# Projecting V as a transposed product and turning it in 32x32 blocks on VectorE

## The chip, the cores and the metric

The kernel runs on one core of a Trainium2 chip. The metric is the device time of one execution in microseconds. A run is one execution; where several are given, the median is compared. The profile is of one execution.

## The reference

The input is x of 2048 rows (tokens) by 512 features in bf16. The result is two rounds of an attention block A and a token-mixing MLP block B, each with a layer norm in front and a residual sum behind:

```python
x = x + A(layernorm(x), wqkv, wo)
x = x + B(layernorm(x), w1, b1, w2, b2)
x = x + A(layernorm(x), wqkv, wo)
x = x + B(layernorm(x), w1, b1, w2, b2)

def A(x, wqkv, wo):        # 32 heads of 16 features, a window of 256 keys behind each query
    q, k, v = split((x @ wqkv).reshape(B, S, 3, H, Dh))
    scores = einsum("bhqd,bhkd->bhqk", q, k) * Dh ** -0.5
    scores = where(0 <= iq - ik < 256, scores, -1e9)
    return einsum("bhqk,bhkd->bhqd", softmax(scores), v).reshape(B, S, D) @ wo

def B(x, w1, b1, w2, b2):  # mixes over tokens
    u = gelu(einsum("bsd,sf->bdf", layernorm(x), w1) + b1)
    return (einsum("bdf,fs->bds", u, w2) + b2).transpose(0, 2, 1)
```

## The kernel before

All tensors of a round lie in the on-chip memory; weights of B are streamed. The 2048 tokens are 16 tiles of 128, and the attention goes through them in four blocks Q of 512 queries. In a block the 32 heads come in four groups t of eight heads, and a group takes nine steps m. So there are 144 steps in a round, 36 for a block and 9 for a group. One step does three things:

- `emit_scores` (L743): products of 64x64 pieces on TensorE for all eight heads, 512 queries, into two banks of PSUM. Two pairs of banks take turns.
- `emit_exp` (L754, L771): ScalarE writes the exponentials of the two banks to one of five slots of `p_sb`; then VectorE or GpSimd multiplies the stretches at the edge of the window with a triangular mask, `edge`.
- `emit_pv` (L792): products of the slot with V on TensorE. Each piece of V has two columns of ones beside it, so the sums of the softmax come out of the same product.

Around the steps stand jobs: `job_transpose` (L554) makes `xhT`, the normalised x with features on partitions; `job_k` and `job_q` (L565, then L606 on VectorE or L611 on ScalarE) project one group of heads for a whole block in four products of 128x128 by 512 and write a masked copy twice, since two heads share a piece; `job_v` (L659) projects V; `job_normalise` (L835, L842) and `job_outproj` (L708) finish a block. The MLP follows (L931, L977); parts of it (`job_part` and the late half of `job_y`, both L581) are put between attention steps.

V is needed with keys on partitions. `job_v(Q, i)` takes one tile of 128 tokens and all 32 heads. Its keys are handled as four groups of 32, and each group is put on partitions 32a to 32a+31 in a product 32 columns wide, so it consists of 64 small products:

```python
last = e.matmul(acc[32 * a:32 * a + 32, k], lhsT=xhT[:, buf, c, t0:t0 + 32], rhs=wv[:, c, :, a, :],
                start=(k == 0 and c == 0), stop=(k == 3 and c == 3), skip_group_check=True,
                tile_position=(0, 32 * a))
```

The bank then holds V for the tile, and one instruction (`masked`: VectorE L606, or two of ScalarE L611) writes it to `v_all`, twice, each time with the partitions of the other heads set to zero by `even`. The jobs' results other than scores and P times V go through two banks of PSUM, 6 and 7 (`misc_bank`).

The order is fixed by tables written out in the kernel: `ORDER` gives the order in which jobs are made, `BANKS` which of the two banks each takes, and `LINES` the exact order of the instructions on each engine. Semaphores do the rest. The first product of P and V in a block waits for what `v_held(Q)` lists: all four tiles of V of that block.

Of the kernel before, what the change touches and what calls it, by code (L numbers as in the profile page):

```python
# [6 lines left out]
dt = mybir.dt  # L7
# [3 lines left out]
P = 128  # L11
# [18 lines left out]
def _table(*text):  # L30
# [5 lines left out]
    'c-pO0!4`lp2onDPqw7$sUg?l!uS1h^FeoAd$IZCcxtcv+t9kXhHM);~qfow6_xQqT^Xo}4wX1n`Su(*gRlcwNx(bk{aKei+``iKU`E$QuyVvts'  # L36
    'w(s>^P)Z~wimbDAvd6)jpPkI@c<da4Ua)cj`@e^2n!S|i3DnSRo!7T}wJfXoUUwnKS75UHw>BeK0EP')
ORDER = _table(
    'c-jTQ17HvU00h8Cwq47%ZQHhOyS8lGwr$(CZ5wxhK!isy7$FcGp%4xs5f%{<29Xg7Q4s^75fiZy0gVs^aS;pAkpOWJAMua~(U1a(kr2s|6iE<('
    ')JTSuNP|>Ji)_e%^vH~K$cRkHiY&;E+{lT1$br1bg*+&Lq9}y?D2T!+h9WqKk|>ALD1qWAg|euKGANHqsDR3-hN`H78fb=ksEOLBj#{XLy6A}p'  # L40
    '=#D0+kH%<<hG>qCXoHq$f&OTXR%nL~Xp0_bk1iOE&gh0t=#8!zf~Dw-UKofzn1}%wj6n3mBn(9mM&KxBU>HVW5QbwU#$q)lU<}4%9HwF)rehhV'
    'U^ZrA8s=dRW?>=bVgVLmF(zXLmSYu`U?tXIEjD2TPGd9HV<XmK3$|iDc3?NQV;gp2FLq%M4&eYUU_XxFI1b|xj^QL8<1DV>6i(ng&fpv_;u3D-'
    'Dz4x%uHy!7;U@0kA@1TnKHv@>;3b~o1)ktJUg0&!XLyIVc#n_xjyC|m;4?nq8$$CJzTzi-;4l6m4ioYZej_+TF&NV`B+YOP!LW?PFwDa6jK+wJ'
    '%E*kxxQx#DjKP?U#{kA=0w$uEgvpqgDH(xDnVQL&ifNgSDOi}9nT8pdi5Z!bQJ9T6n3dU?i)ERcd6|y|n1}gUkcHTWMOlQ!Se%Vmf+bm+rC5eN'
    'Sf15biRD<4RXB##S(!Cil{HwG^;m%o*?_g!ly%sg_1T1t*_zGRg00w&ZP}6?*_j>Kon6_9eb|k?*^lkni~Tu}gV~ouIDkDF#GxF{VI09h9L;eY'
    '#R(kCNgU5<oXDx1&OpxKOwQtD&gE<_;6hH}d@kl9F5yzH;Bv0wTCU_8uIFlQ;70D`O>W|5-rzFs<s9zgHE!W`ZsR)M=3Q>(E#BcS?&c0|=N=y5'
    'exBwT9^@gO<vE_<DW2p-9_JAr<6)lXQC{W+Ug0I)<9%M`BR=K>KH)>Y=2L#=3%=wlKI3zK<a@s1TfXBLe&8p5=MVlN^o>9Ho4@##e`y8RKZaB='
    'Q6Uscp(TY=7)4N6MN)W0R1`&30>xA`MOQ3ERvZN=hGHw8;wq66D!Gy<gOVw+k}9P#Dz#E5y;3Qiax04pE0eM+r?RVodMdASD8KS3pGv8aifVug'
    's<?`%m`bRmnyZW^s-jA(sw$|8YN)bmtGeoHnrf-O>ZqO?s*xHizFMk@+N-r%sGYK@mD;MK(yD_xDYLq$fO4sudZ?PZs=IorlKQH*YO0_5sJwzy'
    'PJ=Z_!xX5Y8llk|sb-p>&g!r68mCDbqox|7Hkzy{ny#r@uNhjbS(>L6nyCevqxo8>MH;B3TB2oIuHjm#)mp1{+MrRItBu;E&Dx@!+M%u5u3g%u'  # L50
    '+1jVwI-tGUqeI%SgF2#PI;#6Ru2Wj0GditvI<Lbzs}s7UtGb|zx~VI=u4_7}Te_{gx}nRuqlbE;M|z;AdZy>Pr#JebS9+=UdaX}-thbWi>7%~u'
    'g+A+>e(RUM>aYIkhrZ~Kf;*T)7!K($ro;ND5<9%ZIf5fOv?DsIqd2-lIkN3oj^?<I=@^df1dikQ4saqTaSA7NQYUvhr*<-@avG;~O2=~sr*|f2'
    'b}naeMrU(Y=Wr3{aYg5JcIS3J7jl00a~&6OQ5SS^7j{dRbupK88JBkjS8`34a1~c~HP?1k*K%Fgb3-?9V>fa$H+Nn)b$hpR8<%!DcW`TWc3Zb|'
    '3s-hGcXU_RaCi4`Pxo>s_jMol_W%!apa*)G2YZBvdbmfrzDIeq$9jUhILPBY(UUycV?5PUJl!)q#IrotGd;(%y}<Lm(#O5fi+s$Bebm#u*7Ll?'
    '>wLn?e9C9M)F*w~tG(PSyvl35(Yw9go4m&xyx04@#hbm=+q}y=yxj-9)BAnUhkeLLeAX9z&R2ZFmwegheciYG%(s2V_kGU~eACzb*f)IDcm3Rt'
    '{L~Nq(og)tZ~V%y{U4S=?Gg')
# [1054 lines left out]
```

## Time and profile before

| | |
|---|---|
| Three runs | 506.96, 507.89 and 508.72 us; median 507.89 |
| Profiled execution | 508.97 us, of it 507.2 in the span of the profile |
| TensorE (PE), busy | 489.2 us, 96%, 10374 products and as many weight loads |
| VectorE (DVE), busy | 320.3 us, 63%, 615 instructions |
| ScalarE (ACT), busy | 325.3 us, 64%, 396 instructions |
| GpSimd (POOL), busy | 189.2 us, 37%, 390 instructions |
| V products, L659 | 2048 of them, 34.8 us busy |

Times in rows are microseconds, those behind a count ("x26 | 31.5, 1215") are the group's busy time in microseconds and the mean of one in nanoseconds. "PEld" is TensorE's weight load, which runs beside the products. "idle before <- X" is the time that the engine stood still before such an instruction and what ended it; "issue" means that nothing which the profile shows held it. The first attention lies at about 10 to 170 us, the first MLP at 165 to 235, the second attention at 235 to 420, the second MLP after that. The granted clock was 1.00 but for a stretch in the slice from 30 to 40 us, where it was 0.83.

### The profile page before, as it was taken

How to read it: one execution, taken by the hardware profiler on the slowest of the kernel's cores; microseconds unless marked ns; L12 is line 12 of the kernel's file. 1: busy time of each engine (PE TensorE's matmuls, PEld its weight loads, DVE VectorE, ACT ScalarE, POOL GpSimd, SP SyncE). 2: the span in 40 equal slices, each digit the busy share in tenths (PEclk: the TensorE clock that was granted, in tenths of full speed). 3: DMA queues.
4: the chain of work that ended last, by engine and by line, in shares of the span. 5: the costliest groups of instructions: out<-in, count | busy, mean ns of one | idle time of the engine just before them, and what ended most of it. 6: DMA issues, size and time to landing. Idle time of an engine off the chain costs nothing.

```text
span 507.2 us, 23041 instructions
## 1 busy us (share of the span) xinstructions
PE 489.2 (96%) x10374; PEld 288.6 (57%) x10374; DVE 320.3 (63%) x615; ACT 325.3 (64%) x396; POOL 189.2 (37%) x390
## 2 busy tenths in 40 slices
PE   8989999899999999999999998998999999999997
PEld 4655756665676544446665665566556654444444
DVE  7879888789755472257868476777785556342223
ACT  4869999898999514404897568787999871240000
POOL 5856645643745120002564133465473322100000
PEclk9989999999999999999999999999999999999999
DMA  6362212141031555031000320014212356222551
GB/s 207 65 70 63 64 44 69 59 132 45 5 109 54 158 152 145 2 108 40 4 26 5 98 78 17 14 41 125 77 45 70 88 141 197 68 78 70 183 152 52
DMA packets 70769, 40.81 MB, mean 80 GB/s; under 512 B 7056, under 2 KB 69648, under 8 KB 70672
## 3 DMA queue, kind: packets, MB, share of 16 engines
q1 hardware_dynamic: 66800, 39.33, 26.4%
q0 software_dynamic: 3872, 0.02, 1.3%
q8 instruction: 81, 1.33, 1.1%
q14 instruction: 16, 0.13, 0.1%
HBM read 32.51 MB, written 2.10 MB: 68 GB/s over the span
## 4 chain that ended last, share of the span: by engine, by line
PE 84%; DVE 5%; ACT 4%; issue 3%; DMA 1%; POOL 1%; SPq 0%; DVEq 0%; POOLq 0%; ACTq 0%
PE ps L977 14%; PE ps L743 12%; PE ps L931 12%; PE ps L792 10%; PE ps L581 10%; PE ps L565 9%; PE ps L659 6%; PE ps L708 5%; ACT p_sb L754 4%; PE ps L554 2%; PE ps L506 1%; PE ps L835 1%; DVE k_sb L606 1%; DMA w1low<-in_B_w_dram 1%; DVE oT L842 1%
## 5 line engine op out<-in xcount | busy, mean ns | idle before, releaser
L754 ACT ACTIVATE p_sb<-ps 128x1024 bf16<-128x1024 f32 (+8 forms) x288 | 261.8, 974 | 45.0 <-PE ps L743 40.1
L771 POOL TENSOR_TENSOR p_sb<-p_sb,edge 128x256 bf16<-128x256 bf16 (+2 forms) x294 | 138.4, 476 | 161.9 <-ACT p_sb L754 141.7
L743 PE MATMUL ps<-q_sb,k_sb 64*64 64x288 bf16 (+8 forms) x2816 | 109.4, 250 | 6.3 <-issue 3.6
L792 PE MATMUL ps<-p_sb,v_all 64*34 64x288 bf16 (+17 forms) x2816 | 88.5, 246 | 1.1 <-issue 0.5
L743 PEld LDWEIGHTS ps<-q_sb,k_sb 64*64 64x64 bf16 x2816 | 58.3, 106 | 49.9 <-ACT p_sb L754 24.0
L792 PEld LDWEIGHTS ps<-p_sb,v_all 64*34 64x34 bf16 (+1 forms) x2816 | 60.7, 101 | 11.3 <-POOL p_sb L771 2.9
L565 PE MATMUL ps<-xhT,wqkv 128*128 128x512 bf16 x240 | 62.0, 384 | 0.0
L981 DVE SCALAR_TENSOR_TENSOR x_sb<-ps,b2col,x_sb 128x512 bf16<-128x512 f32 x23 | 17.2, 750 | 44.4 <-PE ps L977 44.1
L931 PE MATMUL ps<-xh_sb,w1buf 128*128 128x512 bf16 x192 | 44.8, 379 | 0.0
L771 DVE TENSOR_TENSOR p_sb<-p_sb,edge 128x256 bf16<-128x256 bf16 (+2 forms) x106 | 28.1, 268 | 25.8 <-ACT p_sb L754 22.3
L524 POOL TENSOR_TENSOR rstd<-vare,mhalf 128x4 f32<-128x4 f32 (+1 forms) x17 | 16.6, 976 | 71.6 <-DVE vare L522 47.7
L512 DVE BATCH_NORM_STATS2 stats<-x_sb 128x6 f32<-128x512 bf16 x64 | 42.8, 684 | 0.8
L534 ACT ACTIVATE xh_sb<-x_sb,shift,rstd 128x512 bf16<-128x512 bf16 x18 | 14.2, 808 | 44.2 <-POOL shift L528 29.1
L606 DVE TENSOR_TENSOR k_sb<-ps,half 128x1024 bf16<-128x1024 f32 (+1 forms) x29 | 34.2, 1183 | 10.8 <-PE ps L565 8.0
L977 PE MATMUL ps<-ubuf,w1buf 128*128 128x512 bf16 x168 | 37.7, 379 | 0.0
L606 DVE TENSOR_TENSOR q_sb<-ps,even 128x1024 bf16<-128x1024 f32 (+1 forms) x28 | 33.4, 1196 | 6.5 <-PE ps L565 5.3
L659 PE MATMUL ps<-wqkv,xhT 128*32 128x128 bf16 x2048 | 34.8, 220 | 2.6 <-issue 1.8
L606 DVE TENSOR_TENSOR v_all<-ps,even 128x1024 bf16<-128x1024 f32 x26 | 31.5, 1215 | 6.1 <-PE ps L659 5.7
L977 PE MATMUL ps<-ubuf,oU 128*128 128x512 bf16 x154 | 35.0, 379 | 0.0
L581 PE MATMUL ps<-xh_sb,w1low 64*64 64x512 bf16 x512 | 33.9, 377 | 0.8 <-DMA w1low<-in_B_w_dram 0.8
L938 ACT ACTIVATE ubuf<-ps,b1col 128x512 bf16<-128x512 f32 x28 | 18.8, 686 | 23.7 <-DVE ps L936 14.3
L659 PEld LDWEIGHTS ps<-wqkv,xhT 128*32 128x32 bf16 x2048 | 29.1, 97 | 8.5 <-issue 4.8
(80 smaller groups left out, 499.9 us busy)
## 6 DMA issues: line engine op xcount, KB each, us to landing
w1buf<-in_B_w_dram SPq DMA_DIRECT2D x30, 256.0 KB
w1buf<-in_B_w_dram SPq DMA_DIRECT2D x50, 128.0 KB
oU<-in_B_w_dram SPq DMA_DIRECT2D x18, 256.0 KB
oU<-o SPq DMA_DIRECT2D x16, 256.0 KB
w1low<-in_B_w_dram SPq DMA_DIRECT2D x32, 128.0 KB
xhT<-in_B_w_dram SPq DMA_DIRECT2D x4, 512.0 KB
k_sb<-in_B_w_dram SPq DMA_DIRECT2D x4, 512.0 KB
out_dram<-x_sb SPq DMA_DIRECT2D x15, 128.0 KB
```

What stands on the lines that cost most here:

```text
L512: dve(lambda e: e.bn_stats(stats[:, t, :], x_sb[:, t, :]), 690, prio, reads=[R("x", t)], writes=[R("stats", t)])
L565: last = e.matmul(ps[:, b, :], lhsT=wqkv[:, c, c0:c0 + P], rhs=xhT[:, buf, c, :], start=(c == 0), stop=(c == 3))
L581: last = e.matmul(ps[64 * h:64 * h + 64, banks[r ^ swap], :], lhsT=lhs(r ^ swap, c, rows, 64 * h), rhs=rhs(r ^ swap, c, rows), start=(c == ...
L606: return e.tensor_tensor(dst, src.unsqueeze(2).to_broadcast([P, n, 2, w]), mask[:].unsqueeze(1).unsqueeze(3).to_broadcast([P, n, 2, w]), o ...
L659: last = e.matmul(acc[32 * a:32 * a + 32, k], lhsT=xhT[:, buf, c, t0:t0 + 32], rhs=wv[:, c, :, a, :], start=(k == 0 and c == 0), stop=(k = ...
L708: last = e.matmul(ps[:, b, :], lhsT=oT[:, buf, t, i * P:(i + 1) * P], rhs=wo_sb[:, t, :], start=(t == 0), stop=(t == 3))
L743: last = e.matmul(ps[64 * c:64 * c + 64, 2 * half + r, 32 * i0:32 * i1], lhsT=k_sb[rows, ring, t, kb % 16, :], rhs=q_sb[rows, t, c, 32 * i ...
L754: exps[plan.job] = last_exp[0] = plan.op({ACT: (170 + int(2 * (512 - c0) * 0.84), lambda e: e.activation(p_sb[:, slot, :, c0:512], ps[:, 2 ...
L771: return e.tensor_tensor(v, v, g, op=ALU.mult)
L792: last = e.matmul(ps[64 * r:64 * r + w, B_O + (c ^ r), 32 * i0:32 * i1], lhsT=v_all[rows, pos - 32 * c:pos - 32 * c + w], rhs=p_sb[rows, s ...
L931: r = e.matmul(ps[:, b, :], lhsT=blk[:, sc - 8 * part, (ft % 2) * P:(ft % 2 + 1) * P], rhs=xh_sb[:, sc, :], start=(sc == 8 * part), stop=( ...
L977: r = e.matmul(ps[:, b, :], lhsT=blk[:, turn[n], (st % 2) * P:(st % 2 + 1) * P], rhs=u_at(turn[n]), start=(n == 0), stop=(n == NFT - 1))
```

## The change

`job_v(Q, t)` now takes one group of heads for all 512 tokens of a block, as the K and Q jobs do: four products of 128x128 by 512, with features of V on partitions. VectorE then turns the bank in blocks of 32x32 into a float32 tile `vt`, after which keys lie on partitions, and a second instruction writes the masked double copy from `vt` to `v_all`. It may be on VectorE, ScalarE or GpSimd. So that heads come out in the right places, the columns of V's weights are put in another order once: they are loaded into `ubuf`, and eight copies (`permute_wv`) write them to `wqkv`. `v_all` is laid out by groups of heads, and a PV step waits only for V of its own group (`v_held(Q, t)`). In a block's list of jobs V stands at other places, and three of the four V jobs of a block stand inside that block instead of the one before it. `ORDER`, `BANKS` and `LINES` are new as a whole.

```diff
-        v_all = sb("v_all", [P, 30 + (NV * 8 + 1) * VW])
+        VR = 30 + (2 * NV + 1) * VW
+        v_all = sb("v_all", [P, 4 * VR])
+        vt = sb("vt", [P, 2, 512], dt.float32)
...
+        wv_raw = ubuf[:, 0:4 * D].rearrange("p (c n) -> p c n", c=4)
...
-            load(wqkv[:, :, c * D:(c + 1) * D], w_src[:, :, c * D:(c + 1) * D], 1 << 19, -100, writes=[R("wqkv", c)])
+            part = wqkv[:, :, c * D:(c + 1) * D] if c < 2 else wv_raw
+            load(part, w_src[:, :, c * D:(c + 1) * D], 1 << 19, -100, writes=[R("wqkv", c)] if c < 2 else [R("uT", 0), R("uT", 1)])
...
+        def permute_wv(t, prio):
+            cs = slice(t * P, (t + 1) * P)
+            dst = wqkv[:, :, 2 * D + t * P:2 * D + (t + 1) * P].rearrange("p c (a r d) -> p c a r d", r=2, a=4)
+            src = wv_raw[:, :, cs].rearrange("p c (r a d) -> p c a r d", r=2, a=4)
+            for r in range(2):
+                plan.op({DVE: (260, lambda e, r=r: e.tensor_copy(dst[:, :, :, r], src[:, :, :, r])),
+                         POOL: (560, lambda e, r=r: e.tensor_copy(dst[:, :, :, r], src[:, :, :, r])),
+                         ACT: (390, lambda e, r=r: e.activation(dst[:, :, :, r], src[:, :, :, r], ACTF.Copy))},
+                        reads=[R("uT", 0), R("uT", 1)], writes=[R("wv", t)], prio=prio)
...
-        def job_v(Q, i, prio):
+        def job_v(Q, t, prio):
...
-                for k in range(4):
-                    for c in range(4):
-                        for a in range(4):
-                            t0 = i * P + 32 * k
-                            last = e.matmul(acc[32 * a:32 * a + 32, k], lhsT=xhT[:, buf, c, t0:t0 + 32], rhs=wv[:, c, :, a, :],
-                                            start=(k == 0 and c == 0), stop=(k == 3 and c == 3), skip_group_check=True,
-                                            tile_position=(0, 32 * a))
+                for c in range(4):
+                    last = e.matmul(ps[:, b, :], lhsT=wv[:, c], rhs=xhT[:, buf, c, :], start=(c == 0), stop=(c == 3))
                 return last
...
+            turned = dve(lambda e: e.transpose(vt[:, k, :], ps[:, b, :]), 650, prio, shares=[BK(b)], writes=[R("vt", k)])
+            turned.swap = tuple(turned.deps)
+            g0 = 16 * Q % NV
+            for lo, hi in ((0, min(16, NV - g0)), (min(16, NV - g0), 16)):
...
+                def both(e, dst=dst, src=src, n=n):
+                    return e.tensor_tensor(dst, src.unsqueeze(2).to_broadcast([P, n, 2, DH]),
+                                           even[:].unsqueeze(1).unsqueeze(3).to_broadcast([P, n, 2, DH]), op=ALU.mult)
+
+                def each(e, dst=dst, src=src):
+                    for h in range(2):
+                        last = e.activation(dst[:, :, h], src, ACTF.Copy, scale=even[:, h:h + 1])
+                    return last
+                plan.op({DVE: (80 + 34 * n, both), ACT: (230 + 33 * n, each), POOL: (150 + 52 * n, both)},
+                        reads=[R("vt", k), R("even")], writes=[R("v", t, (g + j) // 4) for j in range(0, hi - lo, 4)], prio=prio)
...
-            order = ["k1", "q1", "v0", "v1", "k2", "q2", "v2", "o0", "k3", "q3", "o1", "v3", "K0", "Q0", "o2", "o3"]
+            order = ["k1", "q1", "v1", "k2", "q2", "v2", "k3", "q3", "o0", "o1", "v3", "K0", "Q0", "V0", "o2", "o3"]
...
-                order = ["k1", "q1", "k2", "q2", "k3", "o0", "q3", "o1", "o2", "o3"]
+                order = ["k1", "q1", "v1", "k2", "q2", "v2", "k3", "o0", "q3", "v3", "o1", "o2", "o3"]
...
-        def v_held(Q):
-            first = 4 * Q - 3 if Q > 0 else 0
-            return [R("pad"), R("ones", 0)] + [R("ones", 129)] * (Q > 0) + [R("v", g % (NV // 4)) for g in range(first, 4 * Q + 4)]
+        def v_held(Q, t):
+            slots = [g % NV for g in range(max(0, 16 * Q - 12), 16 * Q + 16, 4)]
+            return [R("pad"), R("ones", 0)] + [R("ones", 33)] * (Q > 0) + [R("v", t, g // 4) for g in slots]
```

192 lines of the change are left out of this document (99 added, 93 removed).

## The prediction

> **What bounds the kernel now.** I read the chain of work that ended last first, then the busy times by stage, then the waits of TensorE.
>
> ```profile
> span 507.2 us, 23041 instructions
> ...
> PE 84%; DVE 5%; ACT 4%; issue 3%; DMA 1%; POOL 1%; SPq 0%; DVEq 0%; POOLq 0%; ACTq 0%
> ```
>
> TensorE carries 84% of the chain, so the time is its work plus its gaps. The stages that hold the V jobs follow (columns: window, its length, busy us of each engine with the count of instructions, granted clock, DMA share, GB/s).
>
> ```profile
> 40.00:140.00 100.00, 96.98 (x2842) 62.02 (x2843) 85.27 (x147) 92.56 (x107) 56.45 (x112) 1.00 0.21 62
> ...
> 300.00:360.00 60.00, 54.65 (x1760) 36.80 (x1756) 44.66 (x82) 48.16 (x53) 29.25 (x53) 1.00 0.16 45
> ```
>
> In the first attention TensorE, ScalarE and VectorE (97, 93 and 85 of 100 us) are all near their limits, so work moved between them has a price; GpSimd (56) has room. From 300 to 360 us TensorE is at 54.65 of 60 and no other engine is full: those are gaps. The waits of TensorE's loads and products (us in total, times, longest):
>
> ```profile
> PEld ps L743 <- ACT p_sb L754: 24.0, 61, 0.8
> ...
> PEld ps L792 <- POOL p_sb L771: 2.9, 10, 0.4
> ```
>
> ```profile
> PE ps L743 <- issue: 3.6, 3, 1.7
> ...
> PE ps L659 <- issue: 1.8, 4, 0.8
> ...
> PE ps L835 <- issue: 1.2, 1, 1.2
> ...
> PE ps L792 <- issue: 0.5, 1, 0.5
> ```
>
> Two things stand out: scores wait for ScalarE to free their banks, often and briefly; and a few long gaps end by nothing that the profile shows, 3.6 + 1.8 + 1.2 + 0.5 = 7.1 us in nine gaps.
>
> **The products of V.** The slot that a job takes on TensorE is read from the start of its weight loads to the start of the next job's, in the timeline:
>
> ```profile
> 105.03 0.90 PEld L659 LDWEIGHTS ps<-wqkv,xhT 128*32 128x32 bf16 x64
> 106.03 0.21 PEld L743 LDWEIGHTS ps<-q_sb,k_sb 64*64 64x64 bf16 x12
> ...
> 109.40 0.55 PEld L565 LDWEIGHTS ps<-xhT,wqkv 128*128 128x128 bf16 x4 [0.20 <-issue]
> 110.37 0.14 PEld L743 LDWEIGHTS ps<-q_sb,k_sb 64*64 64x64 bf16 x8 [0.42 <-issue]
> ```
>
> ```profile
> 118.97 0.97 PE ps L565 x4
> 119.94 0.86 PE ps L708 x4
> ```
>
> The V job of today takes 1.00 us. A job of four full products, the new form, takes 0.97, or 0.86 where it follows another full-array job (the rows of the chain). A listing of the new program's instructions puts 32 such jobs in place of the old, about nine of them next to another full-array job, either before or after: 32 x 0.03 + 9 x 0.11 = 1.9 us saved. Bounds are 1.0 (no neighbour counts) and 32 x 0.14 = 4.5.
>
> **The gaps called issue.** A V job is 64 loads and 64 products in 1.00 us, the densest code of the kernel. The instruction queue's row (packets, MB, share), and TensorE's products around 307 us in the timeline:
>
> ```profile
> q8 instruction: 81, 1.33, 1.1%
> ```
>
> ```profile
> 304.88 0.57 PE L659 MATMUL ps<-wqkv,xhT 128*32 128x128 bf16 x28
> 305.76 1.58 PE L659 MATMUL ps<-wqkv,xhT 128*32 128x128 bf16 x100 [0.31 <-issue]
> 307.27 0.41 PE L743 MATMUL ps<-q_sb,k_sb 64*64 64x288 bf16 x8
> 307.51 0.61 PE L792 MATMUL ps<-p_sb,v_all 64*34 64x224 bf16 x16
> 307.95 0.19 PE L743 MATMUL ps<-q_sb,k_sb 64*64 64x32 bf16 x4
> 309.49 0.40 PE L743 MATMUL ps<-q_sb,k_sb 64*64 64x288 bf16 x8 [1.35 <-issue]
> ```
>
> 1.33 MB in 81 packets is 16.4 KB each; over 2 x 10374 instructions of TensorE it is 64 bytes an instruction, so a packet brings 256. Between the two gaps here (0.31 and 1.35 us) lie 100 + 8 + 16 + 4 = 128 products, which with their loads are 256 instructions: the second gap falls exactly one packet behind the first. I read both as TensorE waiting for its program. With the change 2 x 2048 instructions become 2 x 128, 18.5% of the stream, and 256 of them no longer go by in two or three microseconds. The gaps beside the normalisation (L835, 1.2) stay, and some in L743 may. I take 4.5 of the 7.1 us, with bounds 0 and 7.1. The Trainium skill, "Runtime: NRT & Kernel Launch", section "Instruction fetch mechanics", says that programs are streamed in 16 KiB blocks and that crossing a block is "mostly hidden" behind the issue of instructions; by it nothing would be gained here, and the sum below would be -0.4 us instead of -4.9. The rows above do not look hidden; the rule is a rival below.
>
> **ScalarE at the start of a round.** These are masks of V that ScalarE does between the first exponentials:
>
> ```profile
> 13.84 1.27 ACT L611 ACTIVATE v_all<-ps,even 128x512 bf16<-128x512 f32 x2 [0.76 <-PE ps L659]
> ...
> 17.32 1.27 ACT L611 ACTIVATE v_all<-ps,even 128x512 bf16<-128x512 f32 x2 [0.29 <-PE ps L659]
> ...
> 20.01 1.29 ACT L611 ACTIVATE v_all<-ps,even 128x512 bf16<-128x512 f32 x2
> ...
> 237.45 1.27 ACT L611 ACTIVATE v_all<-ps,even 128x512 bf16<-128x512 f32 x2 [0.18 <-PE ps L659]
> ```
>
> Four tiles of V had to be there before the first PV; now one group is enough, and in the new order two V jobs instead of four stand ahead of or among the first six steps. ScalarE gives up 1.27 + 1.27 + 1.29 us in the first round and 1.27 in the second; it takes on one V mask (1.27, the same size) and two of the weights' copies in the first. For a copy of 256 elements I allow half a V mask's single instruction, 0.35 (0.695 below): 5.1 - 1.27 - 0.7 = 3.1 us less on ScalarE, where exponentials follow each other closely. The three V jobs taken out of the start come back inside the blocks, so TensorE's own sum doesn't change. I take 2.5 us; bounds 0 (TensorE waits for K and Q instead) and 4.
>
> **VectorE.** The rows for its prices:
>
> ```profile
> L606 DVE TENSOR_TENSOR v_all<-ps,even 128x1024 bf16<-128x1024 f32 x26 | 31.5, 1215 | 6.1 <-PE ps L659 5.7
> ...
> L434 DVE COPY o<-ps 128x512 f32<-128x512 f32 x27 | 18.4, 681 | 0.7 <-PE ps L792 0.3
> ...
> L771 DVE TENSOR_TENSOR p_sb<-p_sb,edge 128x256 bf16<-128x256 bf16 (+2 forms) x106 | 28.1, 268 | 25.8 <-ACT p_sb L754 22.3 <-POOL p_sb L771 2.9
> ...
> L531 DVE TENSOR_SCALAR xh_sb<-x_sb,rstd,shift 128x512 bf16<-128x512 bf16 x22 | 10.9, 513 | 5.0 <-POOL shift L528 5.0
> ...
> L611 ACT ACTIVATE v_all<-ps,even 128x512 bf16<-128x512 f32 x12 | 7.7, 695 | 1.9 <-PE ps L659 1.9
> ```
>
> No row shows a turn of 32x32 blocks. Below stands the plain copy of the same bank to float32, 0.68 us, above the mask that writes twice as much, 1.215. I take 0.68, as it too reads and writes 512 elements once: 32 x 0.68 = 21.8 us (38.9 at the upper bound). The 26 masks of V go, -31.5. By the listing VectorE does 15 of the new masks, worth 13.5 full ones: 13.5 x 1.215 = 16.4. Other work that the new order gives it: masks of K and Q (three full, one half: 4.3), 14 more edge masks (14 x 0.268 = 3.8), four more normalised tiles (2.1), three of the weights' copies (3 x 0.27 = 0.8), two copies of results fewer (-1.4). Together 21.8 - 31.5 + 16.4 + 9.6 = 16 us more, nearly all in the two attentions. At 85 of 100 us this comes to some 90. Banks 6 and 7 come free after 0.68 instead of 1.215, which helps, but V's path gets a link longer, and copies of oU and o, on which the next PV waits, queue longer. I charge 2.5 us; bounds 0 (V is made blocks ahead, and nobody waits) and 8 (half of it shows).
>
> **GpSimd.** The listing gives it 19 of V's masks, worth 14.5 full ones, where it had none, and no step loses its place for them.
>
> ```profile
> L771 POOL TENSOR_TENSOR p_sb<-p_sb,edge 128x256 bf16<-128x256 bf16 x102 | 68.5, 673 | 71.2 <-ACT p_sb L754 70.7
> ...
> L771 POOL TENSOR_TENSOR p_sb<-p_sb,edge 128x64 bf16<-128x64 bf16 x92 | 28.1, 307 | 50.7 <-ACT p_sb L754 43.0 <-DVE p_sb L771 5.7
> ```
>
> From 64 to 256 elements the time grows by 366 ns, 1.91 ns an element; 1024 elements make 0.673 + 768 x 1.91 / 1000 = 2.1 us, 31 us in all. An edge mask queued behind one comes up to two microseconds late, about two steps; five slots of `p_sb` cover most of that. PV waits for GpSimd's edges 2.9 us now; I charge another 1.5, bounds 0 and 6.
>
> **The sum.** -1.9 - 4.5 - 2.5 + 2.5 + 1.5 = -4.9 us, against the profiled execution's 508.97 us (1.8 outside its span): 504.1. That execution lies 1.1 above the median of the three runs, 507.89, so I forecast 503.0.
>
> **The rivals.** *The cover holds.* V is made so far ahead that neither VectorE's nor GpSimd's new work shows: -8.9 us, 499.0. For it: the five slots, and the room on GpSimd. Against: VectorE at 85.
>
> *ScalarE sets the pace.* What TensorE saves it then waits for scores' banks (24.0 us in 61 waits already). Of the first two terms only a third is left (2.1), with 2.5 from the start and 4.0 charged: -0.6, so 507.3.
>
> *The gaps stay.* If issue is not the program's arrival but a wait that the profile doesn't show, they don't go with the instructions: -0.4, so 507.5. The Trainium skill's page on the runtime, named above, stands on this side. The exact spacing of 128 products speaks against this case.
>
> *VectorE and GpSimd lock each other out.* The old mask of V read PSUM and one tensor of the SBUF; the new one reads two tensors of the SBUF, as the edge masks do. Those show this:
>
> ```profile
> L771 DVE TENSOR_TENSOR p_sb<-p_sb,edge x106: 156/226/758, 19.9 to 412.4; 128x256 bf16<-128x256 bf16 x42, 128x64 bf16<-128x64 bf16 x36, 128x128 bf16<-128x128 bf16 x28
> ```
>
> ```profile
> 88.08 0.67 POOL L771 TENSOR_TENSOR p_sb<-p_sb,edge 128x256 bf16<-128x256 bf16 x1
> 88.22 0.68 DVE L771 TENSOR_TENSOR p_sb<-p_sb,edge 128x256 bf16<-128x256 bf16 x1
> ```
>
> VectorE's edge mask takes 0.226 in the median, and up to 0.758 where GpSimd's is under way; at 88.22 us it ends just as if it had waited for the other. Now 34 masks of 1.2 to 2.1 us join in. If each holds the other engine up by half of 1.2 us, that is 20 us, and with half of it in front of a waiting PV +10: 508.97 - 4.9 + 10 - 1.1 = 513.0, slower. The point from which it decides is 4.9 / 34 = 0.14 us of delay for each mask that reaches TensorE. Against it: most edge masks are near the median though GpSimd is busy more than half of the time. The Trainium skill, "SBUF — State Buffer", section "SBUF: two separate sides", states this lock for a VectorE instruction with two SBUF inputs against a GpSimd instruction that reads the SBUF; the row at 88.22 agrees.
>
> That the products would not shrink is no rival: the listing shows them gone.
>
> **How the numbers follow.** The forecast has 0.38 (500.5 to 505.5 us), the cover 0.24, ScalarE 0.13, the gaps 0.07, the lock 0.18. A measurement of this kernel can tell about 0.3%, 1.5 us, so faster means below 506.4: 0.38 + 0.24 + 0.05 from the two cases at 507 = 0.67. The rest of those two, with a little of the lock, makes the same, 0.12; slower is 0.21. The range runs from 496.5, the cover with the upper bound on the gaps (2.6 more than taken), to 510.0, which takes in both cases at 507 and the milder half of the lock.
>
> **What would show it.** The instruction queue should come down from 81 packets to about 66, issue on TensorE's products from 7.1 to under 3 us, V's slot to 0.97 or less. The turn should take at most 0.7 us, GpSimd's V mask 1.8 to 2.2, VectorE's about 1.2; a mean well above that, or edge masks with a much longer median, is the lock. PV's waits for edges should grow by no more than 2 us. If scores' waits for ScalarE grow beyond 28 us, ScalarE has the pace. A time above 510 would mean that the lock or VectorE's load was underrated; one below 496 that the waits of the first and of the fourth block were shortened by more than the start's 2.5 us.

## The result, and the profile after

The changed kernel takes 505.06 us (median of four runs, 504.56 to 505.22), the kernel before beside it 508.23 (four runs, 506.96 to 508.72). The ratio is 0.994, with a 95% interval of 0.9919 to 0.996: faster by about 3 us. The profiled execution took 505.04 us, 503.3 of it in the span.

The page of the changed kernel: span, busy times, chain by engine, and the instruction queue (packets, MB, share).

```profile
span 503.3 us, 19233 instructions
...
PE 486.8 (97%) x8454; PEld 272.3 (54%) x8454; DVE 340.9 (68%) x655; ACT 316.9 (63%) x384; POOL 224.6 (45%) x406
...
q8 instruction: 66, 1.08, 0.9%
...
PE 72%; DVE 11%; ACT 6%; POOL 6%; issue 3%; DMA 0%; SPq 0%; POOLq 0%; ACTq 0%; DVEq 0%
```

The program shrank to the 66 packets foreseen. TensorE's share of the chain fell from 84% to 72%, and VectorE, GpSimd and ScalarE took it over (10% before, 23% now): part of what TensorE saved came back as waiting for others. The waits of TensorE's loads say for whom:

```profile
PEld ps L772 <- ACT p_sb L783: 28.1, 71, 0.7
...
PEld ps L821 <- POOL p_sb L800: 9.6, 26, 0.8
...
PEld ps L821 <- DVE p_sb L800: 3.8, 8, 1.3
```

L821 is PV (L792 before), L772 the scores (L743). PV's waits for edges were 2.9 us for GpSimd and 0.4 for VectorE; they are now 9.6 and 3.8. The products' own waits for the program are down to one row, against 7.1 us in four rows before:

```profile
PE ps L772 <- issue: 0.3, 1, 0.3
```

The stages that hold V, in the columns of the same view of before:

```profile
40.00:140.00 100.00, 96.16 (x2290) 54.91 (x2292) 90.50 (x156) 92.30 (x104) 73.51 (x120) 1.00 0.20 61
300.00:360.00 60.00, 58.80 (x1400) 35.74 (x1392) 48.36 (x98) 53.17 (x64) 32.67 (x55) 1.00 0.19 57
```

The second line is the gain: TensorE is busy 58.80 of 60 us where it had been 54.65, with fewer products. In the first, VectorE went from 85 to 90.5 and GpSimd from 56 to 73.5 us, and TensorE is no fuller than it was.

How far the attention has come at a given time shows where the gain was made and given back. The table is worked out from the ends of ScalarE's 288 exponentials; each difference is to the profiled execution of before, in us. The last two columns are versions told below, under the experiments.

| exponential | before, us | changed | four products, old order | the same with turns |
|---|---|---|---|---|
| 18 | 37.0 | -4.5 | -3.6 | -1.9 |
| 54 | 73.1 | -3.4 | -4.0 | +0.2 |
| 108 | 130.7 | -3.1 | -5.5 | -0.2 |
| 144, end of the first attention | 168.6 | -0.9 | -4.7 | +0.7 |
| 162 | 257.5 | -0.1 | -4.8 | +2.0 |
| 198 | 305.9 | -3.8 | -4.4 | +1.9 |
| 234 | 353.1 | -4.4 | -7.1 | +2.0 |
| 288, end of the second | 414.3 | -6.5 | -8.7 | +1.0 |
| end of the span | 507.2 | -3.9 | -8.6 | +1.0 |

The changed kernel wins 4.5 us in the first 18 steps, loses nearly all of it by the end of the first attention, and wins again in the second. Its last 2.6 us of loss are no delay of the attention: the new order leaves eight output products (L737, 32 instructions) behind the last exponential where the kernel before left five (L708, 20 instructions), so the stretch behind it is longer (95.5 us, 93.0 before). Of the first row 1.3 us belong to before's execution: it had 3.4 us at half clock between 30 and 40 us, and a second execution of the same kernel without that stretch reached step 18 at 35.6, step 144 at 167.6 and the end of its span at 506.8. Beside that one the changed kernel has nothing left at the end of the first attention.

Beside the version with four products in the old order, the changed kernel ends 4.6 us later. It is 4.4 us behind by the ninth exponential of the second attention, and 3.8 of these by the end of the first: what it gives away, it gives away there.

### The profile page after: what moved, and what is told of

Read it like the earlier page. It is cut to its first block, busy times and chain, and to the rows that moved or that the text cites. A ratio compares the mean times of both kernels' runs of the same rounds, so it can differ in the third digit from the quotient of the medians.

```text
span 503.3 us, 19233 instructions
## 1 busy us (share of the span) xinstructions
PE 486.8 (97%) x8454; PEld 272.3 (54%) x8454; DVE 340.9 (68%) x655; ACT 316.9 (63%) x384; POOL 224.6 (45%) x406
## 4 chain that ended last, share of the span: by engine, by line
PE 72%; DVE 11%; ACT 6%; POOL 6%; issue 3%; DMA 0%; SPq 0%; POOLq 0%; ACTq 0%; DVEq 0%
PE ps L1006 14%; PE ps L960 13%; PE ps L589 9%; PE ps L772 9%; PE ps L821 9%; PE ps L573 8%; ACT p_sb L783 6%; PE ps L737 5%; PE ps L672 3%; POOL p_sb L800 3%; DVE stats L520 1%; DVE p_sb L800 1%; DVE k_sb L614 1%; DVE oT L871 1%; POOL spread L1051 1%
## 5 line engine op out<-in xcount | busy, mean ns | idle before, releaser
L800 POOL TENSOR_TENSOR p_sb<-p_sb,edge 128x64 bf16<-128x64 bf16 (+2 forms) x280 | 138.3, 503 | 105.3 <-ACT p_sb L783 90.1
L772 PE MATMUL ps<-q_sb,k_sb 64*64 64x288 bf16 (+8 forms) x2816 | 108.0, 249 | 3.2 <-ACT p_sb L783 2.2
L821 PE MATMUL ps<-p_sb,v_all 64*34 64x288 bf16 (+17 forms) x2816 | 91.3, 246 | 3.8 <-DVE p_sb L800 1.5
L772 PEld LDWEIGHTS ps<-q_sb,k_sb 64*64 64x64 bf16 x2816 | 59.1, 106 | 47.7 <-ACT p_sb L783 28.1
L821 PEld LDWEIGHTS ps<-p_sb,v_all 64*64 64x64 bf16 (+1 forms) x2816 | 59.5, 100 | 20.8 <-POOL p_sb L800 9.6
L573 PE MATMUL ps<-xhT,wqkv 128*128 128x512 bf16 x240 | 61.5, 381 | 0.8 <-DVE k_sb L614 0.6
L800 DVE TENSOR_TENSOR p_sb<-p_sb,edge 128x64 bf16<-128x64 bf16 (+2 forms) x120 | 38.9, 335 | 32.3 <-ACT p_sb L783 25.0
L614 DVE TENSOR_TENSOR q_sb<-ps,even 128x1024 bf16<-128x1024 f32 (+1 forms) x31 | 35.9, 1159 | 5.1 <-PE ps L604 2.7
L614 DVE TENSOR_TENSOR k_sb<-ps,half 128x1024 bf16<-128x1024 f32 (+1 forms) x30 | 35.7, 1194 | 3.1 <-PE ps L573 2.3
L687 POOL TENSOR_TENSOR v_all<-vt,even 128x1024 bf16<-128x1024 f32 (+2 forms) x19 | 29.1, 1534 | 17.2 <-DVE vt L675 15.0
L965 DVE TENSOR_TENSOR ps<-ps,ubuf 128x512 f32<-128x512 f32 x16 | 11.2, 700 | 34.0 <-PE ps L960 34.0
L573 PEld LDWEIGHTS ps<-xhT,wqkv 128*128 128x128 bf16 x240 | 19.4, 98 | 26.2 <-issue 4.0
L672 PE MATMUL ps<-xhT,wqkv 128*128 128x512 bf16 x128 | 33.1, 381 | 0.4 <-DVE q_sb L614 0.3
```

What stands on the lines that cost most here:

```text
L573: last = e.matmul(ps[:, b, :], lhsT=wqkv[:, c, c0:c0 + P], rhs=xhT[:, buf, c, :], start=(c == 0), stop=(c == 3))
L614: return e.tensor_tensor(dst, src.unsqueeze(2).to_broadcast([P, n, 2, w]), mask[:].unsqueeze(1).unsqueeze(3).to_broadcast([P, n, 2, w]), o ...
L672: last = e.matmul(ps[:, b, :], lhsT=wv[:, c], rhs=xhT[:, buf, c, :], start=(c == 0), stop=(c == 3))
L687: return e.tensor_tensor(dst, src.unsqueeze(2).to_broadcast([P, n, 2, DH]), even[:].unsqueeze(1).unsqueeze(3).to_broadcast([P, n, 2, DH]), ...
L772: last = e.matmul(ps[64 * c:64 * c + 64, 2 * half + r, 32 * i0:32 * i1], lhsT=k_sb[rows, ring, t, kb % 16, :], rhs=q_sb[rows, t, c, 32 * i ...
L800: return e.tensor_tensor(v, v, g, op=ALU.mult)
```

## The experiments

**The products alone.** The kernel before, with its order, its tiles of 128 tokens and its masks, but four full products where it had 64 small ones.

```diff
-                for k in range(4):
-                    for c in range(4):
-                        for a in range(4):
-                            ...
+                for c in range(4):
+                    last = e.matmul(ps[:, b, :], lhsT=xhT[:, buf, c, i * P:(i + 1) * P], rhs=wqkv[:, c, 2 * D:3 * D],
+                                    start=(c == 0), stop=(c == 3))
```

> The kernel before, its order and all else kept, but each V job's 64 small products replaced by four full products of the same data (the 128 keys then lie on partitions in another arrangement, so V's place in the result is not the reference's). Theory (the gaps called issue are TensorE waiting for its program, and they cost what they measure): slots 32 x 0.03 = 1.0 us and most of the 7.1 us of gaps go, so the instruction queue falls from 81 packets to 66, issue on TensorE's products to under 1 us, and the time from 508 to 501 to 503. Rival ScalarE: the gaps go, but scores then wait for their banks by as much, ScalarE's waits on L743 rise from 24 us to about 29, and the time is 506 to 508. Rival gaps stay: issue remains near 7 us and the time is 507.

Measured: 499.94 us (499.14 to 500.52, six runs) against 507.38 on the same chip; ratio 0.9838 (0.9806 to 0.9869). So 7.4 us by the medians, and 8.2 by the ratio, lie in the form of the products; the forecast had 1.9 + 4.5 = 6.4 for them, and the theory for this run 501 to 503 us, so the gain was underrated. Its page and its waits:

```profile
q8 instruction: 66, 1.08, 0.9%
...
PE 80%; DVE 6%; ACT 6%; DMA 3%; issue 3%; POOL 1%; SPq 0%; DVEq 0%; ACTq 0%; POOLq 0%
```

```profile
PEld ps L739 <- ACT p_sb L750: 31.8, 79, 0.8
...
PEld ps L788 <- POOL p_sb L767: 4.4, 14, 0.4
...
PE ps L788 <- issue: 0.7, 1, 0.7
PE ps L831 <- issue: 0.3, 1, 0.3
```

Of 7.1 us of program gaps 1.0 is left. Scores' waits for ScalarE rose from 24.0 to 31.8: even the simplest version hands a part of its gain to ScalarE.

**The small products in the new order.** The changed kernel, with its V job made of 64 products again.

```diff
-                for c in range(4):
-                    last = e.matmul(ps[:, b, :], lhsT=wv[:, c], rhs=xhT[:, buf, c, :], start=(c == 0), stop=(c == 3))
+                for n in range(4):
+                    for c in range(4):
+                        for a in range(4):
+                            last = e.matmul(ps[32 * a:32 * a + 32, b, n * P:(n + 1) * P], lhsT=wv[:, c, 32 * a:32 * a + 32],
+                                            rhs=xhT[:, buf, c, n * P:(n + 1) * P], start=(n == 0 and c == 0), stop=(n == 3 and c == 3),
+                                            skip_group_check=True, tile_position=(0, 32 * a))
```

> The changed kernel, with each V job's four full products written as 64 small ones (32 columns by 128) that give the same bank; nothing else differs. Theory: the instruction queue is back at 81 packets, issue on TensorE's products at 4 to 7 us, slots 1.0 to 1.9 us longer, and the time goes from 505 to 510 to 513. Rival (the gain of the change lies in the order and in the waits for V, not in the number of instructions): 505.5 to 507.

Measured: 509.83 us (508.05 to 512.4, twelve runs), ratio 1.0048 (1.0024 to 1.0071): 4.8 us more than the changed kernel's median, 5.5 by the ratios; the theory had begun at 510.

```profile
q8 instruction: 81, 1.33, 1.1%
```

```profile
PE ps L674 <- issue: 0.9, 1, 0.9
PE ps L776 <- issue: 0.6, 2, 0.3
...
PE ps L589 <- issue: 0.3, 1, 0.3
```

The packets are back at 81 and the time is back, but only 2.2 us of it stands as gaps before products, where 4 to 7 had been expected. Without the product form the rest of the change makes the kernel slower, by 0.24 to 0.71%.

**VectorE's load in the old order.** The version of the first experiment, with a turn of a bank's size from one scratch tile to another behind each of VectorE's 26 masks of V.

```diff
+            mask = plan.ops[-1]
+            mask.turn = dve(lambda e: e.transpose(vt[:, 0], vt[:, 1]), 650, prio, reads=[R("zero")], writes=[R("vt")])
```

> The version with four full products of V and the old order and masks (ratio 0.984 to the kernel before, 7.4 to 8 us faster), with a turn of a bank's size (512 columns of float32, 0.70 us, from one tile of the on-chip memory to another that nobody reads) behind each of the 26 masks of V that VectorE does: 18.2 us more on VectorE and nothing else, which brings it to about 338 us of busy time, as much as the changed kernel's 341. Theory, VectorE's load alone is a good part of what the changed kernel lost against that version (5 us): the time comes back by 2 to 4 us, ratio 0.988 to 0.992. Rival, the load is hidden and the loss lies with the form of the masks, GpSimd and the new order: ratio 0.983 to 0.986, PV's waits for edges 5 to 7 us together as in that version.

Measured: 509.98 us (509.2 to 510.47, six runs); ratio 1.0071 (1.0048 to 1.0094). Both sides missed: beside the version without turns the time is 10.0 us longer by the medians, 9.5 by the spans and 11.8 by the ratios, on different chips, and not 2 to 4. Its page, its turns and its waits (74 of TensorE's 8454 products are missing from this trace, so its busy time reads low):

```profile
PE 477.1 (94%) x8380; PEld 268.4 (53%) x8454; DVE 337.9 (66%) x642; ACT 325.9 (64%) x396; POOL 189.2 (37%) x390
...
PE 66%; DVE 22%; issue 4%; ACT 4%; POOL 2%; DMA 2%; SPq 0%; DVEq 0%; POOLq 0%; ACTq 0%
```

```profile
L682 DVE STREAM_TRANSPOSE vt<-vt x26: 711/712/714, 16.1 to 367.1; 128x512 f32<-128x512 f32 x26
```

```profile
PEld ps L673 <- DVE xhT L448: 3.6, 6, 0.9
...
PEld ps L808 <- DVE p_sb L787: 2.6, 4, 1.0
PEld ps L851 <- DVE k_sb L623: 2.5, 2, 1.3
```

VectorE's share of the chain went from 6 to 22%. 18.5 us of turns (26 x 0.712) bring 10.0 us of time, 0.54 us each microsecond, at a busy share of 66%. The waits that grew are for what queues behind a turn: the copies to `xhT` (0.9 us without turns), edges (0.9), and K's masks (0.4), which hold a bank that the normalisation wants. With as much on VectorE (340.9 us) the changed kernel is faster than this one by 4.9 us by the medians and 6.6 by the ratios, on different chips. So its new order, with 19 of V's masks moved to GpSimd, earns back about half of what the turns cost in the old one; how much of that is the order and how much the moved masks, these two runs don't separate.

**The copies of V made short in the second attention.** The changed kernel, in its second round with a turn of 32 columns instead of 512 and, on VectorE and GpSimd, masks of two pieces of V instead of up to 32 (ScalarE's too); then the same for GpSimd's masks alone.

```diff
-            turned = dve(lambda e: e.transpose(vt[:, k, :], ps[:, b, :]), ...)
+            tw = 32 if prio > 300 else 512
+            turned = dve(lambda e: e.transpose(vt[:, k, 0:tw], ps[:, b, 0:tw]), ...)
...
-                def both(e, dst=dst, src=src, n=n):
+                def both(e, dst=dst, src=src, n=n, short=False):
+                    if short:
+                        dst, src, n = dst[:, 0:2], src[:, 0:2], 2
```

> The changed kernel, but in the second round of attention alone the turn handles 32 of 512 columns and every mask of V two of its up to 32 pieces; the rest of V keeps what the first round left. The first round is the control within the run. Theory (VectorE's and GpSimd's new work is what ate the gain: waits of PV for edge masks rose from 3.3 to 13.4 us): the second round loses half of that, and the time falls by 4 to 6 us, to 499 to 501. Rival as I had charged it: half of 4.0 us, 503. Rival (their work is hidden, scores wait for ScalarE instead): less than 1 us, 504 to 505.

> The changed kernel, but in the second round GpSimd's masks of V write two of their up to 32 pieces; the rest of V keeps what the first round left. With everything of V's shortened in the second round the time fell to about 502. Theory (GpSimd's masks are most of the price): 502 to 503. Rival (VectorE's turn and masks are): 504.5 to 505.

Measured: all copies short 502.05 us (501.64 to 502.34, six runs; ratio 0.9882, 0.9854 to 0.991), GpSimd's alone 503.88 (503.78 to 504.28, six runs; 0.9912, 0.9889 to 0.9935). Against 505.06 that is 3.0 and 1.2 us for one of two rounds, each between its theory and its rival, so that neither stands as it was put. The forecast had charged 2.5 + 1.5 = 4.0 for both rounds. The busy times of the two (the second trace lacks 75 of the products):

```profile
PE 485.5 (97%) x8454; PEld 271.9 (54%) x8454; DVE 324.3 (65%) x655; ACT 314.9 (63%) x384; POOL 212.2 (42%) x406
```

```profile
PE 476.1 (95%) x8379; PEld 272.3 (54%) x8454; DVE 338.3 (67%) x655; ACT 316.5 (63%) x384; POOL 215.9 (43%) x406
```

With all copies short VectorE has 14.0 us less to do than with GpSimd's alone short (324.3 and 338.3), and the time is 1.8 us shorter (1.5 by the ratios): some 0.13 us each microsecond, far from the 0.54 of the turns in the old order. The first attention, where the table shows the loss, was not shortened, so what the copies cost there is not known.

**The lock.** The rival's mechanism is in the trace of the changed kernel. In the timeline (start, duration), a mask of V on GpSimd and an edge mask on VectorE:

```profile
136.84 1.89 POOL L687 TENSOR_TENSOR v_all<-vt,even 128x1024 bf16<-128x1024 f32 x1
136.92 1.86 DVE L800 TENSOR_TENSOR p_sb<-p_sb,edge 128x64 bf16<-128x64 bf16 x1 [0.17 <-POOL p_sb L800]
```

VectorE's edge masks take 0.278 us in the median (below); this one, of the smallest form, lasts until GpSimd's instruction is done. The Trainium skill's "SBUF — State Buffer", section "SBUF: two separate sides", says that whichever starts first has the shared port for its whole instruction; this pair agrees. The question is what it costs. The new masks read two tensors of the on-chip memory. They can be written as two instructions instead, each with one such input and a column of `even` as a scalar for each partition, so that they are no longer of the form with two inputs.

```diff
-                    return e.tensor_tensor(dst, src..., even..., op=ALU.mult)
+                    for h in range(2):
+                        last = e.tensor_scalar(dst[:, :, h], src, even[:, h:h + 1], None, op0=ALU.mult)
+                    return last
```

First for VectorE and GpSimd both:

> The changed kernel, but VectorE and GpSimd mask V in two instructions of half the size, each with one SBUF tensor and a scalar for each partition instead of two SBUF tensors. Same result. Theory of the lock (an instruction of VectorE with two SBUF tensors and one of GpSimd hold each other up): VectorE's V mask no longer stretches (today 1.68 at most against 1.22), edge masks stretch only against each other, PV's waits for edges fall from 13.4 to 9 to 11 us, time 502 to 504. Rival (plain queueing behind long masks): GpSimd's mask takes 2 x 0.81 = 1.6 us instead of 1.9, the waits fall by 1 us at most, time 504 to 505. Rival (two instructions cost more than one): VectorE's mask over 1.3 us, time 505 to 507.

Measured: 514.13 us (513.79 to 515.93), ratio 1.0127 (1.0096 to 1.0157), 9 us slower than the changed kernel and beyond all that was expected. The masks, by tile, and one wait:

```profile
L688 POOL TENSOR_SCALAR v_all<-vt,even x38: 598/1560/1598, 32.8 to 384.5; 128x512 bf16<-128x512 f32 x22, 128x128 bf16<-128x128 f32 x10, 128x384 bf16<-128x384 f32 x6
L688 DVE TENSOR_SCALAR v_all<-vt,even x30: 268/486/886, 17.1 to 388.9; 128x512 bf16<-128x512 f32 x22, 128x384 bf16<-128x384 f32 x6, 128x128 bf16<-128x128 f32 x2
```

```profile
PEld ps L822 <- POOL p_sb L801: 18.7, 33, 1.8
```

On GpSimd the pair takes 2 x 1.56 = 3.1 us where one instruction took 1.89, and PV waits 18.7 us for its edges. On VectorE the pair is cheaper: 2 x 0.486 = 0.97 us for 1.22. So next only VectorE's masks in that form; then, on top of it, all 19 of GpSimd's masks moved to VectorE, each behind its turn; then only the four of them that had held an edge mask longest.

```diff
+        for o in [o for o in line["gpsimd"] if o.turned]:
+            line["gpsimd"].remove(o)
+            line["vector"].insert(line["vector"].index(o.turned) + 1, o)
```

> The changed kernel, but VectorE alone masks V in two instructions with one SBUF tensor each (0.49 us each in the run before this one); GpSimd keeps its one instruction with two. Same result. Theory (VectorE's work for V and its collisions with GpSimd cost part of the gain): 15 masks get 0.25 us shorter, nothing stretches to 1.68, and the time falls by 1 to 2 us against the changed kernel, to 503 to 504. Rival (GpSimd's long masks in front of its edge masks are the whole price): no change, 505. Rival (the edge masks' own collisions): VectorE's edge masks stay at a mean of 0.33 us and the time at 504.5 to 505.

> As the run before it, and GpSimd's 19 masks of V are moved to VectorE, each right behind its turn, in the form of two instructions. GpSimd has no work of V's left. Same result. Theory (GpSimd's masks of 1.9 us keep edge masks waiting, and collide with VectorE's): PV's waits for GpSimd fall from 9.6 to about 4 us, VectorE's edge masks to a mean of 0.27 us, and although VectorE takes 14 us more, the time falls to 500 to 503. Rival (VectorE, at 90 of 100 us in the first attention, is the price): PV's and K's waits for VectorE rise by more than GpSimd's fall, time 506 to 510.

> The changed kernel with VectorE's masks of V in two one-input instructions, as in the run that gave 502.55 us, and four of GpSimd's 19 masks of V moved to VectorE, each right behind its turn: the four beside which an instruction of VectorE stretched to 1.6 to 1.9 us there. Same result. Theory of the lock (an instruction of VectorE that starts just after GpSimd's mask waits for all of it): no instruction of VectorE of this kind lasts over 1.1 us any more, VectorE's edge masks come down from a mean of 0.32 to about 0.27 us, and the time falls by 0.5 to 2 us against the one-input kernel, to 500.5 to 502. Rival (VectorE's load is the price, as when all 19 were moved): 0.5 to 2 us more, 503 to 504.5. Rival (those stretches hold nobody up): no change.

> The kernel with VectorE's masks of V in two one-input instructions, on the same chip as the run before it, for the comparison: 502 to 503 us, and a ratio to the kernel before of 0.986 to 0.991.

| version | us (range) | ratio to before on its chip |
|---|---|---|
| VectorE's masks with one input | 502.55 (501.59 to 502.87) | 0.9882 (0.9856 to 0.9907) |
| the same, another chip | 501.87 (501.46 to 502.33) | 0.9919 (0.9903 to 0.9934) |
| and all of GpSimd's masks to VectorE | 508.15 (507.82 to 509.6) | 0.999 (0.9974 to 1.0006) |
| and only four of them | 502.17 (501.89 to 502.79) | 0.9925 (0.9908 to 0.9942) |
| the changed kernel, on the chip of the second and fourth row | 504.68 (504.25 to 505.25) | 0.997 (0.9959 to 0.9981) |

The edge masks on VectorE (min/median/max ns), in the changed kernel, with the four masks moved, and with all moved:

```profile
L800 DVE TENSOR_TENSOR p_sb<-p_sb,edge x120: 144/278/1871, 16.5 to 406.9; 128x64 bf16<-128x64 bf16 x44, 128x256 bf16<-128x256 bf16 x41, 128x128 bf16<-128x128 bf16 x35
```

```profile
L810 DVE TENSOR_TENSOR p_sb<-p_sb,edge x120: 144/242/983, 16.5 to 404.3; 128x64 bf16<-128x64 bf16 x44, 128x256 bf16<-128x256 bf16 x41, 128x128 bf16<-128x128 bf16 x35
```

```profile
L809 DVE TENSOR_TENSOR p_sb<-p_sb,edge x120: 144/226/621, 17.0 to 411.4; 128x64 bf16<-128x64 bf16 x44, 128x256 bf16<-128x256 bf16 x41, 128x128 bf16<-128x128 bf16 x35
```

With VectorE's masks in the one-input form the time falls by 2.8 us on the same chip, more than the theory had. The trace shows where. The edge masks on GpSimd, in the changed kernel and in that version, and PV's wait for them there (9.6 us in the changed kernel):

```profile
L800 POOL TENSOR_TENSOR p_sb<-p_sb,edge x280: 293/427/1502, 17.1 to 407.9; 128x256 bf16<-128x256 bf16 x54, 128x64 bf16<-128x64 bf16 x51, 128x128 bf16<-128x128 bf16 x35
```

```profile
L805 POOL TENSOR_TENSOR p_sb<-p_sb,edge x280: 293/427/724, 17.1 to 404.3; 128x256 bf16<-128x256 bf16 x54, 128x64 bf16<-128x64 bf16 x51, 128x128 bf16<-128x128 bf16 x35
```

```profile
PEld ps L826 <- POOL p_sb L805: 6.6, 19, 0.5
```

In the changed kernel seven of GpSimd's edge masks last 0.89 to 1.50 us, each beside a mask of V on VectorE; with the one-input form none is over 0.73. This is the lock the other way round, VectorE holding GpSimd. VectorE's masks of V are also 1.8 us shorter in all (16.0 against 17.8), which these runs don't separate from it. The one-input form is not free of the lock: one such mask on VectorE, 0.49 us in the median, lasts 1.62 us beside a mask of V on GpSimd.

Moving the four takes the 1.87 us stretches away (the version that it starts from has them too, up to 1.873 us). TensorE's longest wait for an edge of VectorE falls from 1.3 to 0.6 us, and the time stays where it was (502.17 beside 501.87), though VectorE and GpSimd both are busy for less (334.9 and 211.7 us, against 336.9 and 218.3). Moving all 19 brings the median back to before's 226 ns and costs 5.6 us, as its rival had it (506 to 510). The busy times and a wait of that version (its trace lacks 75 of the products):

```profile
PE 478.5 (94%) x8379; PEld 274.4 (54%) x8454; DVE 343.3 (68%) x708; ACT 316.7 (62%) x384; POOL 191.0 (38%) x387
```

```profile
PEld ps L576 <- DVE k_sb L617: 3.1, 5, 1.0
```

That version's VectorE (343.3 us) has 6.6 us more than with the one-input masks alone (336.7): the moved masks bring 14.4 us, and the edge masks take 7.9 less. TensorE now waits 3.1 us for banks that K's masks hold, 1.2 with the one-input masks alone; the rest of the 5.6 us is not located. So the lock is real in both directions. Taking away its longest hits on VectorE gained nothing, and taking away VectorE's hold on GpSimd came with up to 2.8 us.

**The best version.** The changed kernel with VectorE's masks of V as two one-input instructions is the fastest that does the whole computation: 502.55 and 501.87 us on two chips, on the second 2.8 us under the changed kernel beside it.

> The changed kernel, unchanged, on the same chip as the two runs before it: 504.5 to 505.5 us, and a ratio to the kernel before of 0.992 to 0.996.

> The kernel before, unchanged, profiled a second time, to see which of its gaps and which stretch of lower clock come back. If the gaps called issue are the program's arrival they stand at the same products, in sum 6 to 8 us. The stretch of half clock at 30 us (3.4 us long) either comes back, and then belongs to the kernel, or not, and then 1.7 us of the difference between the two profiles at the start are the execution's.

The changed kernel's repeat gave a smaller gain than expected (0.997, 1.6 us), as the kernel before ran at 506.3 on that chip. The repeat of before (508.56 us) served its trace: of the seven gaps over 0.3 us that end in issue six stand at the same products as in the first execution, which a chance of the run would not do. The stretch at half clock did not come back.

## Why the prediction was right or wrong

The forecast was 503.0, the result 505.06: the right side, and inside the range. Part of the nearness is luck: the products gave 1 us more than they were put at, and all the rest together cost about 5 us (4.6 by the spans, 5.1 by the medians, beside the version with only the products changed) where -2.5 + 4.0 = +1.5 had been charged. By the steps:

- **The products of V (-1.9) and the gaps called issue (-4.5).** The mechanism is shown: 66 packets, gaps from 7.1 to 0.3 us, and the form of the products alone is worth 7.4 us in the old order and 4.8 in the new. What the gaps wait for is settled by the packets themselves, which the trace of before records. Packets of the instruction queue landed at 304.31, 308.02, 348.39 and 352.61 us; TensorE ended its gaps at 305.76, 309.49, 349.75 and 353.88, before the next packet came. All seven gaps over 0.3 us end 1.3 to 1.6 us behind a landing, and six of them form three pairs that lie 128 weight loads apart. The two gaps that are left in the old order with four products end 1.5 and 1.6 us behind a landing too. The slot is as read: in the changed kernel the next job's loads start 0.97 us behind V's (timeline).

```profile
114.35 0.55 PEld L672 LDWEIGHTS ps<-xhT,wqkv 128*128 128x128 bf16 x4 [0.20 <-issue]
115.32 0.14 PEld L772 LDWEIGHTS ps<-q_sb,k_sb 64*64 64x64 bf16 x8 [0.42 <-ACT p_sb L783]
```

  The size was off in the step "I take 4.5 of the 7.1 us": 6.8 went. The rival "the gaps stay" has fallen, and with it what the forecast drew from the rule that crossing a block of the program is "mostly hidden" (the Trainium skill, "Runtime: NRT & Kernel Launch", section "Instruction fetch mechanics"): most of the 81 packets leave no gap here, but the nine gaps cost 7.1 us.
- **ScalarE at the start of a round (-2.5).** Not settled. At step 18 the changed kernel is 0.9 us ahead of the version with only the products changed (-4.5 and -3.6). But the new order with the small products reaches step 18 at 32.4 us too, 3.2 us before the second execution of before (35.6). So the start is worth 0.9 or 3.2 us, by which of the two changes is taken first. In the second round there is nothing: from the last exponential of the first attention to the ninth of the second it was 80.5 us, now 81.1.
- **VectorE (+2.5).** The durations held (turn 0.705 us foreseen as 0.68, masks 1.22). The load rose by 20.6 us instead of 16, as the edge masks take 38.9 us instead of 28.1, where 3.8 more had been foreseen. The weak step is the price: "I charge 2.5" is 0.16 us for a microsecond of load. The runs show no single price. It was 0.54 for turns in the old order, near the upper bound "half of it shows"; 5.6 us for the 14.4 us of masks moved from GpSimd, 0.39 each; and 0.13 in the second attention of the changed kernel, as low as the forecast had it. The reason given for the lower bound, that V is made blocks ahead, is true of V and misses what is queued behind V's copies on the same engine: copies to `xhT`, K's masks and edges, which TensorE waits for in the rows above. In the first attention, where the changed kernel loses 3.8 us against the version with only the products changed, and VectorE is busy for 90.5 us of 100, its price was not tried: that VectorE's load is the cause there is argued, not shown.

```profile
L675 DVE STREAM_TRANSPOSE vt<-ps x32: 680/705/718, 15.9 to 379.5; 128x512 f32<-128x512 f32 x32
L687 POOL TENSOR_TENSOR v_all<-vt,even x19: 611/1892/2179, 33.2 to 374.9; 128x1024 bf16<-128x1024 f32 x11, 128x256 bf16<-128x256 f32 x5, 128x768 bf16<-128x768 f32 x3
L687 DVE TENSOR_TENSOR v_all<-vt,even x15: 412/1224/1684, 17.1 to 380.2; 128x1024 bf16<-128x1024 f32 x11, 128x768 bf16<-128x768 f32 x3, 128x256 bf16<-128x256 f32 x1
```

```profile
L800 DVE TENSOR_TENSOR p_sb<-p_sb,edge 128x64 bf16<-128x64 bf16 (+2 forms) x120 | 38.9, 335 | 32.3 <-ACT p_sb L783 25.0 <-POOL p_sb L800 6.6
```

- **GpSimd (+1.5).** The mask is 1.89 us where 2.1 was worked out from edge masks, 29 us in all instead of 31. Making the second round's short saved 1.2 us; the first was not tried. PV's waits for GpSimd's edges grew by 6.7 us and for VectorE's by 3.4, 10.1 together and far over the "no more than 2 us" of the forecast. They are not all lost time: TensorE waits less elsewhere.
- **The rivals.** "The cover holds" (499.0) has fallen. "ScalarE sets the pace" holds in part: scores wait 28.1 us for it, 31.8 in the version with only the products, as its mark of 28 foresaw; but that version still gained 7.4. "The lock" is right in mechanism, and the sum had put nothing for it. Its price is up to 2.8 us, by VectorE's masks with one input, and not the +10 of the rival; its costly side is GpSimd's edges held by VectorE's masks, and the reverse gained nothing when four cases were taken away. The chances of the rivals don't add up as told: of 0.20 for the two cases at 507, 0.05 counts as faster, and the 0.15 that are left don't fit into the 0.12 for the same.
- **The sum.** -7.4 for products and gaps stands beside -3.2 measured, both by the medians. Of the 4 to 5 us between them the runs place 3.0 on V's copies in the second attention and up to 2.8 on the lock, which overlap, and leave the first attention open. These parts come from different versions and need not add up.

Two things stay open. The small products in the new order cost 4.8 us with 2.2 us of visible gaps; the rest is not located. And what loses 3.8 us in the first attention, V's copies or the new order itself, was not tried apart.

## What to carry to other kernels

Count TensorE's instructions as well as its columns: 64 small products and their loads in a microsecond use up half a packet of program, and gaps one packet apart, each ending just behind a packet's landing, are the sign that its arrival is the limit. When work moves to an engine at 60 to 70% of the span, price it by what is queued behind it in each stage, and not by the work's own deadline: here a microsecond cost from 0.13 to 0.54 us, by order and stage. And price the form too: a mask as two one-input instructions gained 2.8 us on VectorE, where it no longer held GpSimd's edge masks up, and with GpSimd's masks in that form too the kernel was 9 us slower than without.

## What the hardware showed that was not expected

- A masked copy from float32 to bf16 as two one-input instructions takes 2 x 0.486 us on VectorE against 1.22 for one with two inputs, but 2 x 1.56 on GpSimd against 1.89.
- A turn of 512 columns in 32x32 blocks takes the same from PSUM (0.705 us) as between two tiles of the on-chip memory (0.712).
- An edge mask on VectorE that started 0.08 us behind a GpSimd mask took 1.86 us, until that one was done, and yet taking such cases away did not move the time. The other way round, GpSimd's edge masks beside VectorE's masks of V took up to 1.50 us (0.427 in the median), and the form that ended this came with 2.8 us.
- TensorE's long gaps for its program ended 1.3 to 1.6 us behind the landing of a 16 KB packet of the instruction queue.
